# Polysketch attention and an ELU MLP: batch 2's x as products of 64 rows, and the keys' features of batches 2 and 3 in the runs of the queries

## The chip, the cores and the metric

The kernel runs on one core of a Trainium2 chip. The time is that of one execution on the device, in microseconds (us). Profiles show the same execution engine by engine: TensorE (PE) for matmuls, VectorE (DVE), ScalarE (ACT), GpSimd (POOL), and the queues that issue transfers, SyncE's (SP) above all.

## The reference

Four batches, four heads, 1088 tokens, 32 values a head; everything is fp32. Attention is linear: each key and query is turned into 64 features, the outer product of two projections with 8 values each.

```python
def phi(x):                               # S1, S2: 8 x 32
    a = einsum('rd,bhsd->bhsr', S1, x)
    b = einsum('rd,bhsd->bhsr', S2, x)
    return einsum('bhsi,bhsj->bhsij', a, b).reshape(..., 64)

q_p, k_p = phi(q), phi(k)
kv  = einsum('bhsf,bhsd->bhfd', k_p, v)
z   = sum(k_p, axis=2)
num = einsum('bhsf,bhfd->bhsd', q_p, kv)
den = einsum('bhsf,bhf->bhs', q_p, z)[..., None] + 1e-06
x   = (num / den) as 4352 tokens x 128     # (B*S, H*D)
h   = x @ w_in                             # 128 x 2048
out = where(h > 0, h, exp(min(h, 0)) - 1) @ w_out   # 2048 x 128
```

## The kernel before

**Stages.** Each batch's keys become features (`KF`), their outer products (`KO`, `KO_a`, `KO_b`), and the sums over the tokens `kv` and `z` (`KA`, `Z`). `KT_out` sends `kv` through DRAM into the layouts in which the queries need it: `kvs` (32 rows a tile, the two halves of the features apart) or `kv2` (64 rows a tile). The queries become features (`q1`, `q1_out`), are multiplied and divided by the denominator (`q2_...`), are turned (`q4`), and give x by a product with `kv` (`q5`, `q5_out`).

**The MLP.** The tokens are worked in units `g` of 512 (0 to 7; the last, 8, has 256). Units 2 and 3 are called group 2, 4 and 5 group 4, 6 and 7 group 6; group 8 is the small rest. For each unit there are eight steps `cp` over w_in's columns: `mm1` (L259, tile `h`, two halves of 128 columns), `elu_a` on ACT (L930 RELU, L932 EXP), `elu_d` on DVE (L938, writes `gg`), then the second product, `mm2` for unit 0 and `mm2_seven` (L839) from unit 1 on. `mm2_seven` forms a 2x2 block product from seven products instead of eight; the sums that it needs of `gg` are made by POOL (`sums7`, L795, L800, L802), those of the weights once by `weights7`. Column tiles are 32 wide at first and 64 wide once `width[0] = 64` is set.

**Queries beside the MLP.** `queries(g5s, g1s, step)` takes the two `h` tiles of a step `(unit, cp)` before the step's own `mm1` needs them, and two more PSUM banks, and puts into the four of them x of the groups `g5s` and the features of the groups `g1s`. A group in `pairs` has its x made by `q5_pairs` (L738): 16 matmuls on tiles of 64 rows x 32 columns with `kv2`, from a tile of queries that `q4` has turned on DVE and exchanged between partitions with eight DMAs for each of its halves. Any other group has it made by `q5` (L726): two times 16 matmuls on tiles of 32x32 that add up (f = 0, 1), one half of the features each; a `q1` of the same run stands between them. `q1` (L574) is 16 matmuls on 32x32 tiles. Reading the banks is left to `q5_out` (ACT, L749) and `q1_out` (DVE, L589).

**Keys' features.** `KF_late` (L366) makes those of one batch as eight matmuls on 64x32 tiles with 288 columns each, in two banks of their own; `KF_late_out` (L376) turns each bank with one DVE transposition of 288 columns. Batches 2 and 3 are made in one place, one of them in the two `h` tiles of a step.

**Order.** It is written out by hand, some 880 lines of calls. Each engine executes its instructions in the order in which these calls record them; an instruction waits by semaphores for what it reads, and for a buffer to come free. From unit 6 on, a loop writes the rest. The PSUM tiles `h` have four buffers, two a step.

The calls around the places that are moved, before: group 2's queries and x, and the keys' features.

```python
queries((), (2,), (1, 4))
...
queries((2,), (), (2, 0))
...
queries((), (4, 8), (3, 1))
...
queries((4,), (6,), (3, 7))
```

Of the kernel before, what the change touches and what calls it, by code (L numbers as in the profile page):

```python
# [29 lines left out]
def kernel(  # L30
# [326 lines left out]
    def KF_late(b, step=None):  # L357
        if step is None:
            ps = [psum.tile([P, 512], F32, name="kfps", tag="aux") for _ in range(2)]
        else:  # L360
            ps = hs[step] = [psum.tile([P, 512], F32, name="h", tag="h", bufs=4) for c in range(2)]
        for c in range(4):
            u, w = divmod(c, 2)
            for g2 in range(2):
                r = slice(64 * g2, 64 * g2 + 64)
                nc.tensor.matmul(ps[g2][32 * c:32 * c + 32, :32 * KT],  # L366
                                 Sxp[r].rearrange("p x c r -> p (x c r)"),
                                 kT[b][r, u * KT:u * KT + KT, 32 * w:32 * w + 32],
                                 skip_group_check=True, tile_position=(64 * g2, 32 * c))
        feats[b] = ps  # L370

# [379 lines left out]
    def queries(g5s, g1s, step):  # L751
# [10 lines left out]
        for g, c in keys:  # L762
            q1(g, ps, c, c > 0)
        for g, c in sums:
# [256 lines left out]

    transp(kT, "k", 0, 2, 5)
    KF_first((0, 0), (1, 0))
    KF_first((2, 0), (3, 0))
    transp(kT, "k", 0, KT, KT + 5)
# [3 lines left out]
    transp(kT, "k", 0, 5, KT)  # L1029
    KF_first((5, 0), (3, 1))  # L1030
    KF_first((6, 0), (4, 1))
    KF_first_out(0)
    transp(kT, "k", 0, KT + 5, NT)
    KF_first((5, 1), (7, 0))
    KF_first((6, 1), (8, 0))
    KF_first((7, 1), (8, 1))
    KF_first_out(1)
    KF_first_out(2, slice(1, 2))
    KF_first_out(2, slice(0, 1))
    transp(qT, "q", 0, 0, 8)  # L1040
# [60 lines left out]
    elu_a(0, 0, 0, (0,))
    R1(strip, 4)
    q2_rec(1)
    R1(floor, 4)
    q2_an(1)
    R1(shift, 4)
    whole_half(0, 1)
    R1(whole, 1)
    mm1_first(1, (0, 1))
    elu_a(0, 0, 0, (1,))  # L1110
    q2_out(1, 1)
    mm1(0, 1, (1,))
    mm1(0, 1, (0,))
    q4_early(1, 1)
    R1(round_s, 4)
    q2_out(1, 0)
    elu_d(0, 0, 0)
    elu_a(0, 0, 1, (0,))
    q4_early(1, 0)
    elu_a(0, 0, 1, (1,))  # L1120
    elu_a(0, 1, 1, (0,))
    elu_a(0, 1, 1, (1,))
    elu_d(0, 0, 1)
    R1(whole, 4)
    mm1(0, 2, (0,))
    mm1(0, 2, (1,))
    R1(floor, 2)
    R1(shift, 2)
    R1(round_s, 2)
    q4_out(1, 1)  # L1130
    q4_out(1, 0)
    R1(strip, 7)
    elu_d(0, 1, 1)
    KT_out(0)
    elu_a(0, 1, 0, (0,))
    R1(floor, 3)
    R1(strip, 5)
    R1(whole, 2)
    elu_a(0, 2, 1, (0,))
    elu_a(0, 1, 0, (1,))  # L1140
    q5_early(1)
    q5_early_out(1, 1)
    q5_early_out(1, 0)
    mm2(0, 0, False, (0,))
    R1(shift, 3)
    R1(floor, 5)
    R1(low, 5)
    R1(round_s, 3)
    elu_a(0, 2, 1, (1,))
    R1(shift, 5)  # L1150
    R1(whole, 3)
    weights7(slice(1, 2), 0)
    mm2(0, 0, False, (1,))
    elu_a(0, 2, 0, (0,))
    elu_a(0, 2, 0, (1,))
    elu_d(0, 1, 0)
    R1(floor, 7)
    mm1(1, 0, (1,))
    mm1(1, 1, (0,))
    elu_d(0, 2, 1)  # L1160
    mm1(1, 0, (0,))
    R1(round_s, 5)
    elu_a(1, 1, 0, (0,))
    elu_a(1, 1, 0, (1,))
    R1(strip, 6)
    elu_d(0, 2, 0)
    R1(strip, 8)
    R1(floor, 6)
    R1(shift, 6)
    R1(floor, 8)  # L1170
    R1(round_s, 6)
    R1(whole, 5)
    elu_a(1, 0, 0, (0,))
    elu_a(1, 0, 0, (1,))
    R1(low, 6)
    elu_a(1, 0, 1, (0,))
    R1(shift, 7)
    mm2(0, 1, False, (0,))
    elu_a(1, 0, 1, (1,))
    R1(low, 7)  # L1180
    elu_d(1, 0, 0)
    mm2(0, 1, False, (1,))
    mm2(0, 2, False, (0,))
    mm2(0, 2, False, (1,))
    transp(kT, "k", 1, 9, NT)
    R1(shift, 8)
    R1(round_s, 7)
    mm1(1, 1, (1,))
    elu_a(1, 1, 1, (0,))
    elu_a(1, 1, 1, (1,))  # L1190
    R1(low, 8)
    transp(kT, "k", 1, 0, 9)
    elu_d(1, 0, 1)
    R1(whole, 6)
    mm2_blocks(0, (0,))
    mm1(0, 3, (0,))
    R1(low, 9)
    elu_d(1, 1, 1)
    R1(strip, 9)
    elu_d(1, 1, 0)  # L1200
    KF_late(1, None)
    R1(strip, 10)
    R1(round_s, 8)
    elu_a(0, 3, 0, (0,))
    elu_a(0, 3, 0, (1,))
    elu_d(0, 3, 0)
    R1(whole, 7)
    mm1(0, 3, (1,))
    elu_a(0, 3, 1, (0,))
    mm1(0, 4, (1,))  # L1210
    mm2_blocks(0, (1,))
    elu_a(0, 3, 1, (1,))
    mm1(0, 4, (0,))
    elu_a(0, 4, 0, (0,))
    elu_d(0, 3, 1)
    elu_a(0, 4, 0, (1,))
    KF_late_out(1, 1)
    weights7(slice(2, 4), 0)
    make_SWs()
    R1(floor, 10)  # L1220
    R1(floor, 9)
    R1(shift, 10)
    elu_d(0, 4, 0)
    R1(shift, 9)
    transp(kT, "k", 2, 0, 9)
    R1(round_s, 9)
    mm2(0, 3, False, (0,))
    mm2(0, 3, False, (1,))
    R1(whole, 8)
    mm1(0, 5, (0,))  # L1230
    mm1(1, 2, (1,))
    mm1(0, 5, (1,))
    R1(whole, 9)
    elu_a(0, 4, 1, (0,))
    elu_a(0, 4, 1, (1,))
    elu_d(0, 4, 1)
    KF_late_out(1, 0)
    elu_a(0, 5, 0, (0,))
    KO(1, 0, nc.gpsimd)
    mm2(0, 4, False, (0,))  # L1240
    mm2(0, 4, False, (1,))
    elu_a(0, 5, 1, (0,))
    elu_a(0, 5, 1, (1,))
    elu_d(0, 5, 1)
    elu_a(0, 5, 0, (1,))
    elu_d(0, 5, 0)
    KO_a(1, 1)
    KO_b(1, 1)
    R1(round_s, 10)
    transp(qT, "q", 1, 0, 9)  # L1250
    mm1(0, 6, (0,))
# [24 lines left out]
    elu_a(0, 6, 1, (1,))
    elu_d(1, 2, 1)
    Z_out(1, kv_ps[1])
    Z_share(1)
    elu_d(0, 6, 1)  # L1280
    elu_d(1, 2, 0)
    sums7(1, 2, 0)
    weights7(slice(1, 2), 2)
    mm1(0, 7, (0,))
    elu_a(0, 7, 0, (0,))
    elu_a(0, 7, 0, (1,))
    mm2(0, 6, False, (0,))
    mm2(0, 6, False, (1,))
    mm1(0, 7, (1,))
    transp(kT, "k", 3, 0, 9)  # L1290
    elu_a(0, 7, 1, (0,))
    elu_d(0, 7, 0)
    sums7(1, 1, 1)
    weights7(slice(0, 1), 0)
    weights7(slice(1, 2), 3)
    sums7(1, 1, 2)
    transp(kT, "k", 3, 9, NT)
    queries((), (2,), (1, 4))
    mm1(1, 3, (0,))
    q1_out(2, (2,))  # L1300
    mm2(0, 7, True, (0,))
    q1_out(2, (1,))
    weights7(slice(4, 8), 0)
    elu_a(0, 7, 1, (1,))
    elu_d(0, 7, 1)
    q1_out(2, (3,))
    mm2(0, 7, True, (1,))
    mm1(1, 4, (1,))
    q1_out(2, (0,))
    q2_prod(2)  # L1310
    elu_a(1, 3, 0, (0,))
# [4 lines left out]
    fin1(0)
    q2_sum(2)
    sums7(1, 2, 1)
    weights7(slice(4, 8), 2)
    q2_rec(2)  # L1320
    elu_a(1, 4, 1, (0,))
    q2_an(2)
    mm1(1, 6, (1,))
    mm1(1, 4, (0,))
    elu_a(1, 3, 1, (1,))
    elu_d(1, 3, 1)
    elu_a(1, 4, 0, (0,))
    mm2_seven(1, 1, True, False)
    q2_half(2, 0)
    elu_a(1, 4, 0, (1,))  # L1330
    elu_d(1, 4, 0)
    weights7(slice(2, 4), 3)
    elu_a(1, 4, 1, (1,))
    elu_d(1, 4, 1)
    weights7(slice(2, 4), 2)
    weights7(slice(4, 8), 1)
    mm1(1, 6, (0,))
    elu_a(1, 6, 0, (0,))
    elu_a(1, 6, 1, (0,))
    elu_a(1, 6, 0, (1,))  # L1340
    elu_a(1, 6, 1, (1,))
    sums7(1, 2, 2)
    mm2_seven(1, 2, False, False)
    mm1(1, 5, (0,))
    mm1(1, 5, (1,))
    sums7(1, 3, 0)
    sums7(1, 3, 1)
    q2_half(2, 1)
    weights7(slice(4, 8), 3)
    elu_a(1, 5, 0, (0,))  # L1350
    elu_a(1, 5, 1, (0,))
    elu_a(1, 5, 1, (1,))
    elu_d(1, 6, 1)
    sums7(1, 3, 2)
    elu_d(1, 6, 0)
    sums7(1, 4, 0)
# [617 lines left out]
```

## Time and profile before

| | us |
|---|---|
| three runs | 259.96, 260.21, 260.28; median 260.21 |
| the profiled execution | 260.24, its span 258.3 |
| PE busy | 251.9 (98%) |
| POOL, ACT, DVE busy | 183.9, 182.1, 175.6 |
| first product of the MLP starts | 16.10 |
| TensorE's granted clock | 1.0 throughout |

The span is the time between the first and the last instruction of the profile; 1.9 us of the measured time lie outside of it. Busy times of the engines overlap. PE's is modelled at its ends, so that neighbouring matmuls overlap in the views by some tenths of a us; the chain of waits shows them without the overlap.

### The profile page before, as it was taken

Reading aid. Unit: us, or ns where it says so; the run is one execution under the profiler, and the core shown is the slowest. Engines: PE = TensorE matmul, PEld = TensorE weight load, DVE = VectorE, ACT = ScalarE, POOL = GpSimd, SP = SyncE. Lnnn points to the kernel's source line nnn. Section 1 sums busy time; section 2 is a strip of 40 time slices with the busy share of each in tenths; the row PEclk is TensorE's granted clock in tenths of the full one; section 3 lists DMA queues with packets and bytes.
Section 4 is the critical chain, followed back from the end, with each engine's and each line's share of the span. In section 5 each row is a group of like instructions: output and inputs, shape, how many; then the busy total and the mean of one; then the engine's idle time right before and its main releaser. Section 6 shows DMA issues by size and latency. Waiting matters only on the chain.

```text
span 258.3 us, 9815 instructions
## 1 busy us (share of the span) xinstructions
PE 251.9 (98%) x4133; PEld 160.0 (62%) x4133; DVE 175.6 (68%) x342; ACT 182.1 (70%) x357; POOL 183.9 (71%) x236
## 2 busy tenths in 40 slices
PE   8789999999999999999999999999999999999994
PEld 7643333426666677567566666666766666667994
DVE  5799998898859875789665678743455445644641
ACT  2589887748757657667687777578777777777792
POOL 5433365698994978875779877987888888888310
PEclk9999999999999999999999999999999999999999
DMA  6999692303000111100110004321021100110021
GB/s 187 288 348 248 203 279 59 93 20 52 14 5 4 22 26 27 24 5 5 25 18 3 3 1 95 86 43 28 12 30 25 20 3 0 22 24 3 3 32 31
DMA packets 30427, 15.61 MB, mean 60 GB/s; under 512 B 22544, under 2 KB 28048, under 8 KB 30384
## 3 DMA queue, kind: packets, MB, share of 16 engines
q1 hardware_dynamic: 29520, 14.22, 23.2%
q10 hardware_dynamic: 800, 0.71, 1.0%
q8 instruction: 32, 0.52, 0.8%
q14 instruction: 11, 0.09, 0.1%
q0 software_dynamic: 64, 0.07, 0.1%
HBM read 11.31 MB, written 2.36 MB: 53 GB/s over the span
## 4 chain that ended last, share of the span: by engine, by line
PE 95%; DMA 2%; issue 1%; ACTq 1%; DVE 0%; ACT 0%; DVEq 0%
PE h L259 46%; PE pb L839 18%; PE pa L839 15%; PE o L259 5%; PE ol L259 3%; DMA hd_q<-in_q_dram 2%; PE kv L453 1%; PE qtp L640 1%; PE h L574 1%; PE h L726 1%; PE pb L815 1%; PE xps L666 1%; PE kv L439 1%; PE kfps L366 1%; PE h L738 0%
## 5 line engine op out<-in xcount | busy, mean ns | idle before, releaser
L938 DVE SCALAR_TENSOR_TENSOR gg<-e,h 128x512 f32<-128x512 f32 x128 | 85.4, 683 | 59.7 <-ACT e L932 42.2
L259 PE MATMUL h<-xg,W 128*32 128x512 f32 (+2 forms) x768 | 121.5, 584 | 0.7 <-DVE xg L678 0.7
L930 ACT ACTIVATE e<-h 128x512 f32<-128x512 f32 x128 | 75.0, 591 | 52.4 <-PE h L259 50.4
L795 POOL TENSOR_TENSOR tt<-gg 128x512 f32<-128x512 f32 x55 | 71.6, 1301 | 26.6 <-DVE gg L938 21.1
L932 ACT ACTIVATE e<-e 128x512 f32<-128x512 f32 x128 | 79.0, 630 | 3.0
L259 PEld LDWEIGHTS h<-xg,W 128*32 128x32 f32 (+1 forms) x768 | 34.2, 119 | 44.4 <-issue 32.2
L800 POOL TENSOR_TENSOR tt<-tt,gg 128x256 f32<-128x256 f32 x55 | 41.7, 759 | 3.1
L802 POOL TENSOR_TENSOR tt<-gg,tt 128x256 f32<-128x256 f32 x55 | 40.7, 744 | 3.1
L839 PEld LDWEIGHTS pa<-gg,W 128*64 128x64 f32 (+1 forms) x528 | 25.8, 125 | 25.5 <-issue 25.2
L839 PE MATMUL pa<-gg,W 128*64 128x128 f32 (+1 forms) x528 | 32.4, 273 | 0.0
L839 PE MATMUL pb<-tt,SS 128*64 128x128 f32 (+1 forms) x472 | 29.5, 273 | 0.0
L145 POOL TENSOR_TENSOR W<-W,raw 128x256 uint32<-128x256 uint32 (+2 forms) x12 | 11.7, 978 | 20.0 <-DVE W L119 8.3
L839 PE MATMUL pa<-tt,SS 128*32 128x128 f32 (+1 forms) x404 | 25.3, 273 | 0.0
L839 PEld LDWEIGHTS pb<-tt,SS 128*64 128x64 f32 (+1 forms) x472 | 22.7, 127 | 0.0
L839 PE MATMUL pb<-gg,SS 128*64 128x128 f32 (+1 forms) x292 | 21.9, 273 | 0.0
L839 PE MATMUL pb<-tt,W 128*64 128x128 f32 (+1 forms) x292 | 21.9, 273 | 0.0
L839 PEld LDWEIGHTS pa<-tt,SS 128*32 128x32 f32 (+1 forms) x404 | 17.0, 120 | 0.0
L259 PE MATMUL o<-gg,W 128*32 128x512 f32 x128 | 15.3, 593 | 0.0
L839 PEld LDWEIGHTS pb<-gg,SS 128*64 128x64 f32 (+1 forms) x292 | 13.9, 124 | 0.0
L839 PEld LDWEIGHTS pb<-tt,W 128*64 128x64 f32 (+1 forms) x292 | 13.9, 124 | 0.0
L991 DVE SCALAR_TENSOR_TENSOR gg<-e,h 128x256 f32<-128x256 f32 x16 | 6.6, 418 | 6.4 <-PE h L259 3.2
L259 PEld LDWEIGHTS o<-gg,W 128*32 128x32 f32 x128 | 4.1, 110 | 9.3 <-issue 7.1
(181 smaller groups left out, 273.3 us busy)
## 6 DMA issues: line engine op xcount, KB each, us to landing
raw<-in_moe_w_in_dram SPq DMA_DIRECT2D x8, 256.0 KB, 6.0
raw<-in_moe_w_out_dram SPq DMA_DIRECT2D x8, 256.0 KB, 5.7
out_dram<-ob SPq DMA_DIRECT2D x112, 16.0 KB, 1.5
hd_k<-in_k_dram SPq DMA_DIRECT2D x3, 544.0 KB, 8.5
hd_q<-in_q_dram SPq DMA_DIRECT2D x3, 544.0 KB, 10.0
v<-in_v_dram SPq DMA_DIRECT2D x4, 288.0 KB, 10.0
raw<-qpF SPq DMA_DIRECT2D x16, 64.0 KB, 2.0
v<-in_v_dram SPq DMA_DIRECT2D x3, 256.0 KB, 10.0
```

The source lines that it names most:

```text
L145: nc.gpsimd.tensor_tensor(dst.bitcast(U32), dst.bitcast(U32), words(raw)[0], op=ADD)
L259: nc.tensor.matmul(dst[c:c + tile], lhs[:, c:c + tile], rhs, skip_group_check=True, tile_position=(0, c), **kw)
L366: nc.tensor.matmul(ps[g2][32 * c:32 * c + 32, :32 * KT], Sxp[r].rearrange("p x c r -> p (x c r)"), kT[b][r, u * KT:u * KT + KT, 32 * w:32 ...
L439: nc.tensor.matmul(kv_ps[0][32 * h:32 * h + 32, :R * R], vt[0][:, (h * KT + i) * D:(h * KT + i + 1) * D], feats[0, i // 5][:, i % 5, h].re ...
L795: nc.gpsimd.tensor_tensor(_ap(ts[g, cp][:, 0], [[4 * P, 2], [P, 2], [1, P]]), _ap(gs[g, cp][:, 0, P:], [[4 * P, 2]] + us), _ap(gs[g, cp][: ...
L800: nc.gpsimd.tensor_tensor(t[:, 1], t[:, 2], quarter(g, cp, 0, 0), op=ADD)
L802: nc.gpsimd.tensor_tensor(t[:, 3], quarter(g, cp, 1, 0), t[:, 1], op=SUB)
L839: nc.tensor.matmul(bank[r:r + width[0], P * col:P * col + P], lhs[:, w:w + width[0]], rhs[:, u], start=(first and i in ((0,) if g == 1 els ...
L930: nc.scalar.activation(e, hs[g, cp][c][:, :n], RELU, scale=-1.0)
L932: nc.scalar.activation(e, e, EXP, scale=-1.0)
L938: nc.vector.scalar_tensor_tensor(gs[g, cp][:, c, :n], es[g, cp][:, c, :n], -1.0, hs[g, cp][c][:, :n], op0=ADD, op1=MAX)
L991: nc.vector.scalar_tensor_tensor(gs["last", k // 2][:, k % 2, :2 * P], es["last", k // 2][:, k % 2, :2 * P], -1.0, hs["last", k][:, :2 * P ...
```

## The change

Four things are changed.

1. `pairs` holds group 4 too: batch 2's x is made by `q5_pairs`, and `KT_out` writes no `kvs` for batch 2.
2. `KF_beside` makes the features of batch 3's keys in the run of group 2's queries (step (1, 4)) and those of batch 2's keys in the run of group 2's x (step (2, 0)), in columns 256 and up of the same four banks: 16 matmuls with 160 or 128 columns on 64x32 tiles, in place of eight with 288. `KF_beside_out` turns them in four transpositions instead of two.
3. The queries of groups 4 and 8 are made in the run of step (2, 7) instead of (3, 1).
4. The whole order is written anew. Of what it moves, the text speaks of these: `q4_early(1, 1)` and `q4_early(1, 0)` (the `qtp` transpositions, L640) no longer follow each other on PE but have a `mm1` between them, and so have the two halves of `KA(1)`; `KS_turn` and `KS_out` come earlier at the start; `width[0] = 64` is set before the run of step (3, 7) and not behind it; only one `mm1` stands between that run and `mm1(3, 7, (0,))`.

```diff
-    pairs = (6, 8)
+    pairs = (4, 6, 8)
...
-    kvs = {b: const.tile([P, H, 2, D], F32, name=f"kvs{b}") for b in (1, 2)}
+    kvs = {b: const.tile([P, H, 2, D], F32, name=f"kvs{b}") for b in (1, )}
...
+    def KF_beside(b, ps):
+        feats[b, "kf"] = ps
+        feats[b] = work.tile([P, 2, KT, H, R], F32, name="abk", tag="abk", bufs=2)
+        for c in range(4):
+            u, w = divmod(c, 2)
+            for i in range(4):
+                g2, (t0, t1) = i // 2, ((0, 5), (5, KT))[i % 2]
+                r = slice(64 * g2, 64 * g2 + 64)
+                nc.tensor.matmul(ps[i][32 * c:32 * c + 32, 256:256 + 32 * (t1 - t0)],
+                                 Sxp[r].rearrange("p x c r -> p (x c r)"),
+                                 kT[b][r, u * KT + t0:u * KT + t1, 32 * w:32 * w + 32], start=False, stop=True,
+                                 skip_group_check=True, tile_position=(64 * g2, 32 * c))
+
+    def KF_beside_out(b, i):
+        g2, t = i // 2, (slice(0, 5), slice(5, KT))[i % 2]
+        nc.vector.transpose(feats[b][:, :, t, 2 * g2:2 * g2 + 2, :].rearrange("p x t c r -> p t x (c r)"),
+                            feats[b, "kf"][i][:, 256:256 + 32 * (t.stop - t.start)].rearrange(
+                                "p (t x y) -> p t x y", x=2, y=2 * R))
...
-    def queries(g5s, g1s, step):
+    def queries(g5s, g1s, step, kf=None):
...
             q1(g, ps, c, c > 0)
+        if kf:
+            KF_beside(kf, ps)
         for g, c in sums:
...
+    queries((), (2,), (1, 4), 3)
...
+    mm1(1, 4, (0,))
...
+    mm1(1, 7, (1,))
...
+    queries((2,), (), (2, 0), 2)
+    q5_out(2, 0, 0)
+    q5_out(2, 1, 0)
...
+    KF_beside_out(2, 3)
...
+    mm1(1, 7, (0,))
+    elu_a(1, 7, 0, (0,))
+    q5_out(2, 0, 1)
...
+    KF_beside_out(2, 1)
+    KF_beside_out(2, 0)
...
+    mm2_seven(1, 5, False, False)
+    KF_beside_out(2, 2)
+    mm1(2, 0, (0,))
...
+    queries((4,), (6,), (3, 7))
+    mm1(3, 6, (0,))
...
+    q5_out(4, 0, 0)
+    elu_a(3, 6, 1, (0,))
+    q1_out(6, (0,))
+    mm1(3, 7, (0,))
```

More of the change, by code (lines that the diff above doesn't have):

```diff
@@ L1114 @@
     q4_early(1, 1)
-    R1(round_s, 4)
+    elu_a(0, 0, 1, (0,))
+    R1(low, 2)
+    elu_a(0, 0, 1, (1,))
+    mm1(0, 2, (0,))
+    make_SWs()
     q2_out(1, 0)
-    elu_d(0, 0, 0)
-    elu_a(0, 0, 1, (0,))
+    elu_d(0, 0, 1)
+    q4_out(1, 1)
+    R1(whole, 2)
     q4_early(1, 0)
-    elu_a(0, 0, 1, (1,))
+    R1(floor, 3)
+    R1(strip, 5)
+    elu_a(0, 1, 0, (0,))
+    elu_a(0, 1, 0, (1,))
+    q4_out(1, 0)
+    mm2(0, 0, False, (0,))
+    KT_out(0)
+    mm2(0, 0, False, (1,))
+    R1(floor, 5)
@@ L1121 @@
+    R1(shift, 3)
+    elu_a(0, 2, 0, (0,))
+    R1(strip, 6)
+    R1(low, 5)
+    elu_a(0, 2, 0, (1,))
+    R1(round_s, 3)
+    R1(strip, 7)
+    elu_d(0, 1, 0)
+    q5_early(1)
+    mm1(0, 2, (1,))
+    R1(shift, 5)
+    R1(floor, 6)
+    q5_early_out(1, 1)
+    q5_early_out(1, 0)
+    R1(whole, 3)
+    mm2(0, 1, False, (0,))
+    mm1(1, 1, (0,))
     elu_a(0, 1, 1, (0,))
     elu_a(0, 1, 1, (1,))
[L1123 to L1127, printed above, removed]
@@ L1161 @@
     mm1(1, 0, (0,))
[L1162 to L1181, printed above, removed]
     mm2(0, 1, False, (1,))
     mm2(0, 2, False, (0,))
+    mm1(1, 1, (1,))
@@ L1211 @@
[L1211 to L1227, printed above, removed]
+    elu_a(1, 1, 1, (1,))
+    elu_a(0, 3, 1, (1,))
+    R1(low, 8)
+    weights7(slice(1, 2), 0)
+    R1(round_s, 8)
@@ L1297 @@
[L1297 to L1311, printed above, removed]
+    elu_d(1, 2, 1)
+    transp(kT, "k", 3, 9, NT)
+    transp(kT, "k", 2, 0, 9)
+    elu_d(1, 2, 0)
+    keep_last(1)
+    mm2(0, 6, False, (0,))
@@ L1312 @@
+    elu_a(1, 3, 1, (0,))
+    elu_a(1, 3, 1, (1,))
+    sums7(1, 2, 2)
+    sums7(1, 1, 2)
+    q2_rec(2)
+    elu_d(1, 4, 0)
+    q2_an(2)
+    mm2_seven(1, 1, True, False)
+    elu_d(1, 4, 1)
+    sums7(1, 4, 0)
+    q2_half(2, 1)
+    elu_d(1, 3, 1)
     elu_a(1, 3, 0, (1,))
-    mm1(1, 3, (1,))
-    elu_a(1, 3, 1, (0,))
     elu_d(1, 3, 0)
[L1316 to L1343, printed above, removed]
@@ new lines @@
+    elu_a(2, 5, 1, (0,))
+    KA(3, (1,))
+    sums7(2, 3, 1)
+    Z_share(2)
+    sums7(2, 3, 2)
+    sums7(2, 4, 1)
+    elu_a(2, 5, 0, (1,))
+    elu_a(2, 5, 1, (1,))
+    elu_d(2, 5, 0)
+    elu_a(2, 6, 1, (0,))
+    elu_d(2, 5, 1)
+    mm2_seven(2, 3, False, False)
+    elu_a(2, 6, 1, (1,))
+    elu_a(2, 6, 0, (0,))
+    elu_a(2, 6, 0, (1,))
+    sums7(2, 5, 0)
+    KT_out(3)
+    zls[3] = ZC(3, kv_ps[3])
+    Z(3, kv_ps[3], zls[3])
+    Z_out(3, kv_ps[3])
+    elu_d(2, 6, 0)
+    elu_d(2, 6, 1)
@@ L1649 @@
+    q2_prod(8)
+    q2_an(6)
+    elu_d(3, 7, 1)
     elu_d(3, 7, 0)
-    elu_d(3, 7, 1)
-    sums7(3, 5, 1)
+    mm1(4, 0, (1,))
+    mm1(4, 0, (0,))
+    elu_a(4, 0, 1, (0,))
+    q5_out(4, 1, 1)
     sums7(3, 5, 2)
-    elu_a(3, 6, 0, (0,))
-    mm1(4, 0, (1,))
-    elu_a(3, 6, 0, (1,))
-    elu_d(3, 6, 0)
-    q2_sum(6)
+    mm2_seven(3, 5, False, False)
     sums7(3, 6, 0)
+    elu_a(4, 0, 1, (1,))
+    elu_d(4, 0, 1)
     sums7(3, 6, 1)
-    sums7(3, 7, 0)
-    elu_a(4, 0, 1, (0,))
-    q2_rec(6)
@@ L1738 @@
-    sums7(4, 3, 2)
-    mm1(4, 6, (1,))
-    elu_d(4, 4, 1)
-    q2_sum(8)
+    elu_d(4, 4, 1)
+    elu_d(4, 4, 0)
+    sums7(4, 7, 0)
+    mm1(4, 5, (1,))
+    mm1(4, 6, (1,))
+    elu_a(4, 6, 1, (0,))
+    elu_a(4, 5, 1, (0,))
+    mm1(4, 5, (0,))
+    mm2_seven(4, 3, False, False)
+    mm1(4, 6, (0,))
+    elu_a(4, 5, 0, (0,))
+    sums7(4, 7, 1)
+    fin_seven_c(3)
+    q2_rec(8)
+    q2_an(8)
+    q2_half(8, 0)
+    elu_a(4, 5, 0, (1,))
     sums7(4, 4, 0)
-    elu_a(4, 6, 1, (0,))
-    elu_a(4, 6, 1, (1,))
+    sums7(4, 7, 2)
@@ new lines @@
+    elu_a(5, 3, 0, (0,))
+    sums7(5, 2, 1)
+    sums7(5, 1, 2)
+    mm2_seven(5, 1, False, False)
+    elu_a(5, 3, 1, (0,))
+    elu_a(5, 3, 0, (1,))
+    elu_d(5, 4, 0)
+    elu_d(5, 3, 0)
+    sums7(5, 2, 2)
+    mm2_seven(5, 2, False, False)
+    elu_a(5, 3, 1, (1,))
+    queries((6, 8), (), (5, 7))
+    q5_out(6, 0, 1)
+    q5_out(6, 1, 0)
+    q5_out(8, 0, 0)
+    q5_out(6, 0, 0)
+    q5_out(8, 0, 2)
+    q5_out(8, 0, 1)
+    mm1(5, 5, (1,))
+    elu_a(5, 5, 1, (0,))
+    elu_d(5, 3, 1)
@@ L1848 @@
+    elu_a(5, 5, 1, (1,))
+    sums7(5, 3, 0)
+    sums7(5, 3, 1)
+    sums7(5, 3, 2)
+    mm1(5, 5, (0,))
+    q5_out(8, 0, 3)
+    sums7(5, 4, 0)
+    elu_a(5, 5, 0, (0,))
+    mm1(5, 7, (1,))
+    mm1(5, 7, (0,))
+    mm2_seven(5, 3, False, False)
+    elu_d(5, 5, 1)
+    mm1(5, 6, (1,))
+    elu_a(5, 5, 0, (1,))
+    fin_seven_c(4)
+    elu_d(5, 5, 0)
     sums7(5, 5, 0)
-    sums7(5, 3, 0)
-    queries((6, 8), (), (5, 7))
-    elu_d(5, 4, 0)
+    sums7(5, 4, 1)
+    elu_a(5, 7, 0, (0,))
+    q5_out(6, 1, 1)
```

1063 lines of the change are left out of this document (506 added, 557 removed).

## The prediction

> **What bounds the kernel now.** I read the page's shares and its chain first.
>
> ```profile
> PE 251.9 (98%) x4133; PEld 160.0 (62%) x4133; DVE 175.6 (68%) x342; ACT 182.1 (70%) x357; POOL 183.9 (71%) x236
> ...
> PE 95%; DMA 2%; issue 1%; ACTq 1%; DVE 0%; ACT 0%; DVEq 0%
> ```
>
> TensorE carries the chain. The view of waits, for PE, says whether it ever stands:
>
> ```profile
> PE kv L439 <- issue: 0.8, 1, 0.8
> PE idle L267 <- PEq L1959: 0.8, 1, 0.8
> PE h L259 <- DVE xg L678: 0.7, 1, 0.7
> PE abqp L527 <- DVE qT L285: 0.5, 1, 0.5
> ```
>
> All four lie before the first product of the MLP, which starts at 16.10. From there on PE has no gap. So three things can move the end: the start, what PE loses where the shape of its tiles changes, and new waits. The matmuls are the same work: counted from the two built programs, columns by share of the array, they agree.
>
> The chain (start, us, what) prices a change of shape:
>
> ```profile
> 19.75 1.02 PE qtp L640 x8
> 20.77 1.85 PE h L259 x16
> ...
> 33.66 0.65 PE kfps L366 x16
> ...
> 43.89 1.72 PE h L259 x16
> ...
> 73.19 0.86 PE h L259 x8
> 74.05 0.65 PE kfps L366 x16
> 74.69 0.48 PE h L366 x16
> 75.18 0.99 PE h L259 x8
> ```
>
> Sixteen `h` take 1.72 in a row of their own shape and 1.85 behind another; eight take 0.86 and 0.99. So each return costs 0.13. `qtp` streams as many columns as eight `h` and takes 1.02 instead of 0.86, so entering it costs about 0.16. The runs of `queries` are read in the same way, from the end of one neighbour to the start of the next:
>
> ```profile
> 52.88 0.34 PE h L574 x2
> ...
> 53.54 0.55 PE h L259
> ...
> 70.09 0.34 PE h L726 x2
> ...
> 71.52 0.36 PE pa L839 x8
> ...
> 122.18 0.34 PE h L726 x2
> ...
> 124.24 1.00 PE h L259 x3
> ```
>
> "Bare" below is columns alone, at the rate of the long products (512 columns in 0.86, four 32-wide or two 64-wide tiles at once; the sixteen tiles of 32x32 work together). Group 2's q1, one set of 16 matmuls: 0.66 (bare 0.43). Group 2's x, two sets: 1.43 (bare 0.85). Step (3, 7) with group 4's two sets and group 6's one: 2.06 (bare 1.28). The excess is 0.23, 0.58, 0.78 for one, two, three sets. Step (3, 1), two sets: 104.66 to 105.82, 1.16 (bare 0.53, excess 0.63). Groups 6 and 8 as pairs: 176.31 to 177.71, 1.40 (bare 1.07, excess 0.33), group 6's part 0.88.
>
> **The change, part by part,** from the profiled execution of 260.24 (span 258.3 and 1.9 around it; the median is 0.03 less).
>
> Start. The first KA waits for v's landing, whose issue is not moved; KA is at 10.03 in both. Behind it, KS_turn and KS_out come earlier, so that `xps` (14.70) waits less: about -0.06. ACT's strip(2) now stands ahead of KS_out and waits for a weight that lands at 12.54; about 0.15 us are to spare.
>
> Keys' features. Removed: KF(2)+KF(3), 74.05 to 75.18, 1.13, and the 0.13 of the `h` behind it. Added: in the run of steps (1, 4) a second set (bare 0.43+0.48=0.91), in that of (2, 0) a set between two (bare 1.33), and one and two changes between 32x32 and 64x32 tiles, which the trace does not show. By the excess of two and three sets: 0.91+0.33 to 0.91+0.63 is 1.24 to 1.54, and 1.33+0.58 to 1.33+0.78 is 1.91 to 2.11. An inner change costs between nothing and 0.15 (the `qtp` row). I take 1.50 and 2.20, since a set of another shape must wait for its weights too. Together 3.70 against 0.66+1.43+1.13+0.13=3.35: **+0.35** (-0.20 to +0.75).
>
> Batch 2 as pairs. Step (3, 7) has two sets instead of three: 0.88 (group 6's row) + 0.66 (q1's row) + 0.15 = 1.69 against 2.06: **-0.37** (-0.52 to 0). The widening of the column tiles moves ahead of the run; I take nothing for it, 0.13 at most.
>
> `q4_early(1, ·)` is cut in two by a product: one more entry and one more return, 0.16+0.13: **+0.30**. KA(1) is cut in two; a half behind a product starts about 0.1 late (45.61+0.86=46.47, first `kv` at 46.59): **+0.08**. Steps of q1(4) and q1(8) only change their step: nothing.
>
> The Trainium skill, "TensorEngine Tiling (Array Packing)", Key Properties, says that changing the tiling mode drains TensorE. By that rule the five changes more that I count from the first product on would cost 5 x 0.29/2 = 0.7 by the `qtp` row before anything is saved; the rows above agree that a change costs, and the sum here has them one by one.
>
> Waits that are new. PE stands only if a bank is not read in time, so I walked the outputs of each run.
>
> ```profile
> 71.56 0.37 ACT L749 COPY xg<-qps 128x256 f32<-128x256 f32 x1 [0.52 <-PE qps L726]
> 71.83 0.66 ACT L749 COPY xg<-h 128x256 f32<-128x256 f32 x2
> ...
> 124.27 0.65 ACT L749 COPY xg<-h 128x256 f32<-128x256 f32 x2 [0.76 <-PE qps L726]
> ```
>
> DVE's reading of a bank waits for ACT's reading of the same one (at 124.95 it starts 0.03 behind the copies). In (2, 0), KF_beside_out(2, 1) waits for q5_out(2, 0, 1), and that stands on ACT behind the RELU of mm1(1, 7, (0,)). From that product's end: RELU starts 0.21 later, the copy 0.50 after it and takes 0.39, then two transpositions (0.30 and 0.32, between the 0.21 of 64 columns and the 0.42 of 256, overlapping by 0.06) and 0.12 for two handovers: 1.78. mm1(2, 0, (0,)) needs that bank, and PE gets there after one mm2_seven, 1.50: **+0.28** (0 to 0.5). Queued behind are the ELU of (1, 7) and, through it, mm1(2, 1). In (3, 7) one product instead of two stands between the run and mm1(3, 7, (0,)): copy 0.22 to 0.61 after the run, transposition to 1.08, PE there at 0.98: **+0.13**. In (1, 4) four transpositions fit with 0.3 to spare, and in (5, 7) the copies with 0.3.
>
> Off PE. Batch 2's x now goes through SP: 16 DMAs in q4(4) (the page has 64 KB, 2.0 us each), for four fewer in KT_out(2), which were done long before. SP first issues 16 outputs of fin_seven_c(1) (0.6 each), then eight pieces at 0.45 and, after the other q4(4), eight more: landed about 121.5, needed at 124; 2.3 us of cover. POOL's sums7, 1.36+0.81+0.69 a product from when the ELU is there, keep 0.5 us before their use at the tightest (mm2_seven(5, 4)); that of before keeps 0.4. No cost.
>
> Sum: -0.06+0.35-0.37+0.30+0.08+0.28+0.13 = +0.71, so 260.95; I say **260.9**. 0.2% is 0.52 us, about what a measurement can tell from no change, so 259.7 to 260.7 counts as the same.
>
> **Rivals.**
> *DVE late at 60 to 70 us* (slower still). Its queue from 58.9: q2_rec 0.35, seven ELU writes at 0.65, q2_an 0.5, two products of 1.22, two transpositions of 1.24, one KF output 0.25: 10.6 to 11.3 us. elu_d(1, 5, 1) is ready about 68.8 for mm1(1, 7, (1,)) at 69.5, elu_d(1, 5, 0) at 70.0 for the run at 70.5. Half a microsecond late decides it, and then it is paid one to one, 0.5 to 1.5: 261.4 to 262.4. Against it: PE is itself later by then.
>
> *The sets refill each other's time* (the other side). If the excess is PE waiting for the next set's weights, a set of long passes between two others hides it: then each run keeps one set's 0.23, 0.91+0.23=1.14 in (1, 4) and 1.33+0.23=1.56 in (2, 0), and (3, 7) is 0.88 and a bare 0.43, 1.31: -0.65 and -0.75 instead of +0.35 and -0.37. That is -0.67, and -1.08 if the two bank waits go as well: 259.2 to 259.6. For it: 16 KF matmuls behind 16 others took 0.48 (74.69), bare. Against: those had the same shape.
>
> *The change doesn't do what it says*: KF_beside writes a tile twice in a row, and if matmuls start only in written order, the other tiles stand idle behind it: eight tile turns of about 0.37 instead of 0.48 in all, +2.6 a run, 266. Against it, each matmul here is two passes on one tile, and at 176.24 eight tiles start together though the first one's second pass starts at 176.48.
> The Trainium skill, "TensorE: Matmul & The Clock Gate", Part 2, says that "the MATMULs themselves stay in program order"; by that the 266 would come; the 176.24 row speaks against it.
>
> *q4(4) lands after 124*: each microsecond over the 2.3 is paid, 262 to 263. *The small sizes come out low and the bank waits don't show*: 260.2.
>
> **Numbers.** Forecast (260.5 to 261.4) 0.45, DVE 0.16, refill 0.19, small 0.14, order 0.02, DMA 0.04. Left out are the order case, the lower half of refill, and the far ends of DVE and DMA, some 0.2 in all: 259.4 to 262.2. Faster is refill with a little of small, 0.20; same is the rest of small and a quarter of the forecast, 0.24; slower 0.56.
>
> **What would show it.** After, the runs of (1, 4) and (2, 0) as 1.5 and 2.2 in the chain, (3, 7) as 1.7, a `qtp` of four twice with an `h` between, and in the waits of PE two rows more: `h` on DVE `abk`, about 0.3, and on DVE `abw`, about 0.1. Wrong would be: no such row, or runs near 1.2 and 1.6 (then refill), or a wait on `gg` at 69 (DVE), on `raw` at 124 (DMA).

## The result and the profile after

The changed kernel takes 263.06 us (median of 6 executions, 262.00 to 264.11) beside 260.07 for the kernel before (median of 6, 259.05 to 260.28): a ratio of 1.0126, 95% interval 1.0107 to 1.0145. It is slower, as forecast, but by 3.0 us and not by 0.7, and it lies outside the range of 259.4 to 262.2. A second set of executions of the same kernel (r1 below) gave 1.0145 (1.0120 to 1.0169). Each ratio is to the kernel before as it ran in the same set; it is estimated from the executions and need not be the quotient of the two medians. Some executions run in a slower state of the chip, whatever the kernel (two of r5's ten, one of r8's twelve); medians and ratios leave them out.

The profiled execution took 264.11, the slowest of the six, its span 262.0; the granted clock is 1.0. The page's shares, the chain's shares and the waits of PE, after:

```profile
PE 254.3 (97%) x4133; PEld 163.6 (62%) x4133; DVE 175.6 (67%) x346; ACT 180.6 (69%) x357; POOL 184.6 (70%) x236
...
PE 93%; DMA 2%; DVE 1%; ACT 1%; issue 1%; ACTq 1%; DVEq 0%
```

```profile
PE abqp L546 <- DVE qT L285: 1.0, 1, 1.0
...
PE h L259 <- DVE gg L959: 0.6, 1, 0.6
...
PE pb L860 <- issue: 0.3, 1, 0.3
```

The number of matmuls is the same. PE is still the chain, but DVE and ACT have now a share of it, and there are two waits behind the start that the kernel before does not have. The first product of the MLP starts at 16.03 (before 16.10), so from there to the end of the span it is 245.97 against 242.2: 3.8 us more. All of the loss in this execution is behind the start. In r1's profile of the same kernel the same stretch is 245.2, 3.0 us more than before, so the table below shows a loss on the large side.

The predicted parts can be read from the chain and from PE's timeline. The split `q4_early(1, ·)`, from the chain:

```profile
19.86 0.59 PE qtp L659 x4
20.45 0.99 PE h L259 x8
21.44 0.59 PE qtp L659 x4
22.03 1.85 PE o L259 x16
```

Both `qtp` runs pay their entry and both products behind them their return. The runs with the keys' features, by the first matmul of the run and of what follows it, from PE's timeline (start, us, engine, line, instruction):

```profile
51.49 0.41 PE L593 MATMUL h<-qT,SWs 32*32 32x256 f32 x2
...
52.96 1.07 PE L259 MATMUL o<-gg,W 128*32 128x512 f32 x8
```

```profile
70.55 0.41 PE L745 MATMUL h<-qpT,kvs 32*32 32x256 f32 x2
...
72.67 1.07 PE L259 MATMUL h<-xg,W 128*32 128x512 f32 x8
```

That is 1.47 for (1, 4) and 2.13 for (2, 0). In the same way (3, 7) is 126.67 to 128.48, 1.80.

What the sum did not have is elsewhere. First, step (4, 0), in the chain:

```profile
129.60 0.60 ACT e L951
...
130.49 1.12 DVE abw L608 x3
...
132.10 0.47 DVE den L624
...
132.86 0.64 DVE gg L959
133.54 1.94 PE h L259 x8
```

`mm1(4, 0, (1,))` needs a bank of step (3, 6), which `elu_d(3, 6, 0)` reads. That stands on DVE behind `q1_out(6, ·)`, `q2_prod(6)`, `q2_sum(6)` and `q2_rec(6)`, and those wait for ACT, which copies x only behind the RELU of the product at 128.55. PE loses 0.78. Then the weight loads, whose rows name waits that the view of PE's waits leaves out (PEld is TensorE's loading of weights; in brackets: idle time before the row, and what ended it):

```profile
67.80 0.16 PEld L860 LDWEIGHTS pb<-tt,W 128*32 128x32 f32 x8 [0.24 <-POOL tt L823]
...
75.36 0.19 PEld L259 LDWEIGHTS h<-xg,W 128*32 128x32 f32 x8 [0.36 <-ACT e L953]
...
104.32 0.12 PEld L860 LDWEIGHTS pb<-tt,W 128*32 128x32 f32 x3 [0.51 <-issue]
```

The one at 75.36 is the predicted bank wait of (2, 0), though ACT's EXP is named and not DVE's `abk` (whose transposition ends at 75.25). The other two were not foreseen. And SP, which issues the outputs of unit 3 ahead of the last eight DMAs of `q4(6, 1)`:

```profile
152.00 5.06 SPq L736 DMA_DIRECT2D raw<-qpF  x8
157.16 8.76 SPq L922 DMA_DIRECT2D out_dram<-ob  x16
166.01 4.95 SPq L736 DMA_DIRECT2D qpE<-qpF  x8
171.06 5.96 SPq L736 DMA_DIRECT2D raw<-qpF  x8
```

The last of them is issued by 177.02 and lands at 178.47; the run of (5, 7) goes from 177.43 to 179.49, 2.05 instead of 1.40.

| behind the first product, us | predicted | after |
|---|---|---|
| keys' features (3.35 before) | +0.35 | 1.47+2.13-3.35 = +0.25 |
| run (3, 7) (2.06 before) | -0.37 | 1.80-2.06 = -0.26 |
| `q4_early` cut in two | +0.30 | +0.29 |
| `KA(1)` cut in two | +0.08 | +0.06 |
| bank wait in (2, 0) | +0.28 | +0.28 |
| bank wait in (3, 7) | +0.13 | +0.12 |
| change of width before the run (3, 7) | 0 | +0.11 |
| `mm1(4, 0, (1,))` waits for DVE | - | +0.78 |
| run (5, 7) waits for `q4(6, 1)` | - | +0.65 |
| gap inside `mm2_seven(2, 4)`, at 104 | - | +0.65 |
| gap behind the small `Z` product, at 99 | - | +0.33 |
| `mm1` from 16 to 20, `mm2_seven(1, 3)` waits for POOL | - | +0.18, +0.17 |

The first six come to 0.74, the rest to 2.9, together 3.6 of the 3.8.

Two of these rows hang together. Behind the gap at 104 the four column tiles, 32 columns wide each, are out of step: until the change of width at 124 one of them runs 0.14 ahead of the other three.

```profile
120.65 0.59 PE L259 MATMUL h<-xg,W 128*32 128x512 f32 x1
...
120.79 1.89 PE L259 MATMUL h<-xg,W 128*32 128x512 f32 x15
```

From the first matmul of `mm2_seven(3, 2)` (122.36) to the first 64-wide product (124.14) it is 1.78. In r4, r5 and r12, which have no gap at 104, it is 1.64, and such an `mm2_seven` alone takes 1.53. So the change of width itself costs 0.11, and 0.14 there belong to the gap. From the end of the run of (2, 7) to that product it is 21.78, and 21.13 in r12: the gap costs 0.65 in all.

### The profile page after: what moved, and what is told of

It reads as the page before. It is cut to its first block, busy times and chain, and to the rows that moved or that the text cites. A ratio compares the mean times of both kernels' runs of the same rounds, so it can differ in the third digit from the quotient of the medians.

```text
span 262.0 us, 9850 instructions
## 1 busy us (share of the span) xinstructions
PE 254.3 (97%) x4133; PEld 163.6 (62%) x4133; DVE 175.6 (67%) x346; ACT 180.6 (69%) x357; POOL 184.6 (70%) x236
## 4 chain that ended last, share of the span: by engine, by line
PE 93%; DMA 2%; DVE 1%; ACT 1%; issue 1%; ACTq 1%; DVEq 0%
PE h L259 45%; PE pb L860 18%; PE pa L860 14%; PE o L259 5%; PE ol L259 3%; DMA hd_q<-in_q_dram 2%; PE kv L472 1%; PE qtp L659 1%; PE h L757 1%; PE h L593 1%; PE pb L836 1%; PE xps L685 0%; PE kv L458 0%; DVE abw L608 0%; PE h L745 0%
## 5 line engine op out<-in xcount | busy, mean ns | idle before, releaser
L259 PEld LDWEIGHTS h<-xg,W 128*32 128x32 f32 (+1 forms) x768 | 37.0, 119 | 46.6 <-issue 31.5
L860 PEld LDWEIGHTS pa<-gg,W 128*64 128x64 f32 (+1 forms) x528 | 27.5, 125 | 23.1 <-issue 22.0
L860 PE MATMUL pa<-gg,W 128*64 128x128 f32 (+1 forms) x528 | 33.4, 273 | 0.0
L860 PE MATMUL pb<-tt,SS 128*64 128x128 f32 (+1 forms) x472 | 30.6, 273 | 0.0
L860 PE MATMUL pa<-tt,SS 128*32 128x128 f32 (+1 forms) x404 | 26.4, 273 | 0.0
L860 PEld LDWEIGHTS pb<-tt,SS 128*64 128x64 f32 (+1 forms) x472 | 23.7, 127 | 0.0
L860 PE MATMUL pb<-tt,W 128*64 128x128 f32 (+1 forms) x292 | 23.3, 273 | 0.3 <-issue 0.3
L860 PEld LDWEIGHTS pa<-tt,SS 128*32 128x32 f32 (+1 forms) x404 | 18.1, 120 | 0.0
L259 PE MATMUL h<-xgl,W 128*64 128x128 f32 x128 | 9.4, 273 | 0.0
```

Source lines behind the costliest of these rows:

```text
L259: nc.tensor.matmul(dst[c:c + tile], lhs[:, c:c + tile], rhs, skip_group_check=True, tile_position=(0, c), **kw)
L860: nc.tensor.matmul(bank[r:r + width[0], P * col:P * col + P], lhs[:, w:w + width[0]], rhs[:, u], start=(first and i in ((0,) if g == 1 els ...
```

## Experiments

The theory: the terms of the sum are right, and the rest is a set of separate waits that the new order makes on queues far from the edits, each of which goes away when its one call is put elsewhere. The rivals, run by run: that a wait only moves to the next place, that the loss lies in the edits (pairs, keys' features), or that it lies in the start.

### The changed kernel again

> The changed kernel once more, for a second profile and as the ruler of this set. Theory A (new waits, not the new products, make the time): the same three gaps on TensorE come back, 0.78 us ahead of mm1(4, 0, (1,)) at about 133, 0.65 in the run of step (5, 7) at about 178, and some 0.3 and 0.5 around the run of step (2, 7) at 101 and 104; 262 to 264. Theory B (the profile of the first run caught a disturbed execution): one or more of these gaps is gone, and the time is near 262.

Measured: 263.45, ratio 1.0145 (1.0120 to 1.0169). The wait at (4, 0) is there with 0.79, the run of (5, 7) is 1.80 (0.40 over), the gap in `mm2_seven(2, 4)` 0.31. The gap of 0.33 at 99 is not there: that one is a matter of the execution. So is the 0.18 that `mm1` loses from 16 to 20: r6, in the old order, has it too, and r2, r4, r8, r9 and r11, in the new one, do not.

### fin_seven_c(3) behind q4(6, 1)

```diff
-    fin_seven_c(3)
...
     q4(6, 1)
...
+    fin_seven_c(3)
```

> Only fin_seven_c(3), whose 16 output transfers stand on SyncE's queue ahead of the last 16 transfers of groups 8 and 6, is moved behind them. Theory A: the run of step (5, 7) takes 1.40 us again, as in the kernel before, instead of 2.05; 0.65 less than the changed kernel, about 262.4. Theory B (the run is long because of its products, or TensorE waits for something else there): 2.05 stays, no change of the time.

Measured: 264.18, ratio 1.0163 (1.0112 to 1.0214). SP now takes the exchange first:

```profile
165.72 4.94 SPq L736 DMA_DIRECT2D qpE<-qpF  x8
170.76 6.03 SPq L736 DMA_DIRECT2D raw<-qpF  x8
176.89 5.22 SPq L922 DMA_DIRECT2D out_dram<-ob  x9
```

The run of (5, 7), now from 178.63, takes 1.41. This profile alone does not settle it: the last eight DMAs are issued by 176.79, only 0.2 earlier than in the profile after, while PE comes to the run 1.2 later. r5 below has the same order on SP, and its first product starts at 16.39, near the 16.03 of the profile after:

```profile
168.82 6.18 SPq L736 DMA_DIRECT2D raw<-qpF  x8
```

There they are issued by 175.00, two us earlier, and the run takes 1.41 although PE comes to it earlier, at 176.69: the wait was SP's order. The time of r2 shows nothing of it, and in the profiled execution the start says why. The first product starts at 17.85, 1.8 later than in the profile after (behind it, it is 244.7): PE stands 2.2 for q's first rows, and from 10 to 14 us the clock is granted at 0.73, 0.50, 0.50 and 0.57.

### The denominators of group 6 behind elu_d(3, 6, ·)

```diff
-    q2_prod(6)
-    q2_sum(6)
-    q2_rec(6)
     elu_d(3, 6, 0)
...
     elu_d(3, 6, 1)
+    q2_prod(6)
+    q2_sum(6)
+    q2_rec(6)
```

> Only the three instructions of group 6's denominator (q2_prod, q2_sum, q2_rec: 0.42, 0.45, 0.35 us on VectorE) are moved behind elu_d(3, 6, 0) and elu_d(3, 6, 1). Theory A: TensorE no longer waits ahead of mm1(4, 0, (1,)), 0.6 to 0.8 us less than the changed kernel, about 262.3. Theory B: the wait there has another cause (the copies of ScalarE, POOL's sums) and stays over 0.5.

Measured: 262.57, ratio 1.0122 (1.0096 to 1.0149); in the profile behind the first product 244.7, 1.3 less than after. PE's wait on `gg` is gone, since DVE writes it 1.4 earlier:

```profile
131.43 1.28 DVE L959 SCALAR_TENSOR_TENSOR gg<-e,h 128x512 f32<-128x512 f32 x2
```

Not all of the 1.3 is the edit's: the gap at 99 is missing and (5, 7) waits only 0.22, while the gap in `mm2_seven(2, 4)` was 0.80 here. By the times alone the edit is not told apart from none, since the intervals overlap.

### r4_three_waits: both, and elu_d(2, 6, ·) ahead of Z_out(3)

```diff
-    Z_out(3, kv_ps[3])
     elu_d(2, 6, 0)
     elu_d(2, 6, 1)
+    Z_out(3, kv_ps[3])
```

> Both edits, and elu_d(2, 6, 0) and elu_d(2, 6, 1) ahead of Z_out(3) on VectorE, which waits for TensorE. Theory A: the gaps at (5, 7), (4, 0) and 0.3 at (2, 7) are gone, 1.7 us less than the changed kernel, 261.3, and what is left over the kernel before is near the 0.7 of the prediction plus 0.5. Theory B: less than 0.8 comes back; the rest lies in the products and in the changes of shape.

Measured: 261.66, ratio 1.0072 (1.0048 to 1.0096). This interval lies below that of the changed kernel. The waits at (4, 0) and (5, 7) and the gap at 104 are gone together, and in the profile it is 243.4 behind the first product, 1.1 over the kernel before. So most of the unforeseen 2.9 is these. But the start is late in this profile (first product at 17.74), which gives DMAs time. r5, with the same three edits and a start 1.35 earlier, waits 0.66 in the run of (3, 7): a part of what is removed can come back at the next transfer.

### r12: elu_d(2, 6, ·) ahead of Z_out(3) alone

> The changed kernel with one edit: elu_d(2, 6, 0) and elu_d(2, 6, 1) stand ahead of Z_out(3) on VectorE. Theory A (these two free the banks of step (2, 7), and Z_out(3) holds them 1.45 us while it waits for kv): the gap of 0.33 before the run at 101 is gone, the run starts when the product ahead of it ends, and the gap of 0.3 to 0.8 inside mm2_seven(2, 4) goes with it or moves; behind the first h 0.3 to 0.9 below the changed kernel's 245.97. Theory B (both gaps are TensorE waiting for its instructions): the gaps stay where they are, within 0.1 us of their place, and no difference behind the first h.

Measured: 262.51, ratio 1.0095 (1.0063 to 1.0127); behind the first product 244.6. The loads of `mm2_seven(2, 4)` now follow each other without a gap:

```profile
103.00 0.24 PEld L860 LDWEIGHTS pb<-tt,W 128*32 128x32 f32 x8
103.22 0.24 PEld L259 LDWEIGHTS h<-xg,W 128*32 128x32 f32 x8
```

All five profiles without this edit and with the new order (after, r1, r2, r3, r9) have the gap at the same instruction, 0.3 to 0.8; all six with it (r4, r5, r8, r10, r11, r12) have none. The edit removes it, but how is open. The reason that I gave, the bank that `Z_out(3)` holds up, would put the gap before the run, and it lies behind it, where the profile names no releaser. In the five profiles with the gap, a 16 KB instruction packet on the DMA queues ended 1.30 to 1.48 before PE went on, however long the gap was; in the six without it, PE came to the same instruction 1.73 to 2.23 behind the end of such a packet. That PE waits there for its instructions fits both, and is only argued. The gap at 99 is another thing: it was gone here, but r10 and r11 have it with the same edit (0.33 and 0.40), so the edit is not what took it away.

### r5_start_order: the start as before

r4 with `q1_first` again between the calls of `Z_first`, and `q1_first_out` and `q2_out(0, 1)` again behind `zl` and `Z_out`.

> The changed kernel with the three edits of the run before, and TensorE's order at the start put back: the sums of the first keys (Z_first) stand around the queries' first products (q1_first) instead of behind them, and the copy zl on ScalarE ahead of the copy of the queries' features. Theory A (the start hangs on the landing of hd_q since the change, with no time to spare, and where that is late TensorE's clock falls too): the first product of the MLP starts at 16.1 or earlier in the profile, no clock below 1.0 between 10 and 14 us, and the median is 0.4 to 1 us below the run with the three edits, about 261.0. Theory B (the start varies for reasons that the order has no part in): no difference, 261.7.

Measured: 262.1, ratio 1.0078 (1.0052 to 1.0104), against r4's 1.0072. No gain. In the profile, (3, 7) took 2.46: PE comes there at 126.09, and the last DMA of group 4's exchange lands at 127.07 (after: 126.67 and 126.90).

### r9_start_both: the start alone

```diff
-    q1_first(0, 1)
-    q1_first(2, 3)
-    q1_first_out()
     Z_first(0, 1, 2)
+    q1_first(0, 1)
     Z_first(3, 4, 5)
     Z_first(6, 7, 8)
+    q1_first(2, 3)
...
-    q2_out(0, 1)
...
     Z(0, feats["z"], zl)
...
+    q1_first_out()
+    q2_out(0, 1)
...
-    R1(strip, 4)
...
     q5_early_out(0, 1)
+    R1(strip, 4)
```

> The changed kernel with only the start put back: Z_first around q1_first as before, zl ahead of the copy of q1_first, and R1(strip, 4) behind q5_early_out(0, 1). Theory A (the start has no slack against the landing of q's first rows, so in some executions TensorE stands about 2 us and the granted clock then falls to a half): first h at 15.4 to 16.1, no slice of the clock below 0.9 before it, kv x40 at 0.70, and a ratio 0.3 to 0.8 us (0.001 to 0.003) below that of the changed kernel (1.0126 and 1.0145), while the waits behind the start stay: behind the first h 245 to 246. Theory B (the start varies as much in the order of before): same ratio as the changed kernel within 0.0015.

Measured: 263.28, ratio 1.0124 (1.0092 to 1.0157), that of the changed kernel. Theory A falls: with this order too, PE stood 2.2 for q's first rows, the first product started at 16.67, and this time the clock stayed at 1.0. Over all profiles the transposition of those rows starts between 6.8 and 8.4, in both orders. The start scatters with their landing, and it is not where the change loses.

### r6_pairs_only: the kernel before with pairs = (4, 6, 8)

```diff
-    pairs = (6, 8)
+    pairs = (4, 6, 8)
...
-    kvs = {b: const.tile([P, H, 2, D], F32, name=f"kvs{b}") for b in (1, 2)}
+    kvs = {b: const.tile([P, H, 2, D], F32, name=f"kvs{b}") for b in (1, )}
```

> The kernel before with group 4 in pairs and nothing else: batch 2's x in products of 64 rows, in the old order. Theory A (this part gains what its row says): the run of step (3, 7) takes 1.80 instead of 2.06, and the kernel is 0.2 to 0.3 us faster than before. Theory B (16 transfers more on SyncE's queue cost what the products gain): the run waits for the exchanged queries, and the kernel is as before or slower by up to 1 us.

Measured: 268.66, ratio 1.0337 (1.0299 to 1.0375). In the old order the exchange lands far too late, and PE waits for it:

```profile
PE h L738 <- DMA raw<-qpF: 3.6, 1, 3.6
...
PE qps L738 <- DMA raw<-qpF: 1.1, 2, 0.7
```

The 3.6 lie ahead of the run: it begins at 125.79, before at 122.11. Then it takes 6.03 instead of 2.06, with the clock granted at 0.66, 0.50 and 0.50 in the 2 us windows from 126 to 132, and the four products behind it take 4.45 instead of 3.58. That is 8.5 of the 8.8 that it takes longer behind the first product. SP issues the exchange from 116.91 to 128.04. So this rival, the DMAs of `q4(4)`, is real and large; only the new order, in which group 4's queries and their exchange come earlier, keeps it away.

### r7_beside_only: the kernel before with KF_beside in the two runs

```diff
-    queries((), (2,), (1, 4))
+    queries((), (2,), (1, 4), 3)
...
-    queries((2,), (), (2, 0))
+    transp(kT, "k", 2, 9, NT)
+    queries((2,), (), (2, 0), 2)
...
-    transp(kT, "k", 2, 9, NT)
-    KF_late(2, None)
-    KF_late(3, (2, 1))
```

> The kernel before with the keys' features of batches 3 and 2 in the runs of steps (1, 4) and (2, 0) and nothing else. Theory A (this part costs what its rows in the changed kernel say): the runs take 1.47 and 2.13, the run of 1.13 at 74 and its return of 0.13 are gone, so 0.27 slower than before, if VectorE's transpositions are in time. Theory B (the products beside the queries gain, and it is the new order alone that costs): 0.3 us faster than before or more.

Measured: 260.35, ratio 1.0028 (1.0004 to 1.0052), the four `KF_beside_out` placed behind the runs. Behind the first product 242.6, 0.3 over the kernel before; the runs take 1.55 and 2.13. So the profile bears out the predicted +0.35 by itself; the times alone put it between 0.1 and 1.4.

### r8_all_waits: r5 and five small edits

```diff
-    mm1(0, 2, (0,))
...
     q4_early(1, 0)
+    mm1(0, 2, (0,))
...
-    weights7(slice(4, 8), 3)
...
     sums7(1, 3, 2)
+    weights7(slice(4, 8), 3)
...
     q5_out(2, 1, 0)
+    q5_out(2, 0, 1)
...
-    q5_out(2, 0, 1)
...
-    width[0] = 64
...
     queries((4,), (6,), (3, 7))
+    width[0] = 64
...
-    mm1(3, 7, (0,))
...
     mm2_seven(3, 4, False, False)
+    mm1(3, 7, (0,))
```

> The run with the old start, and six smaller edits of the order: q5_out(2, 0, 1) ahead of the RELU of (1, 7); mm1(3, 7, (0,)) behind mm2_seven(3, 4); the two q4_early(1, ·) together again; weights7(slice(4, 8), 3) behind sums7(1, 3, ·); the widening of the column tiles behind the run of (3, 7). Theory A (the loss is a list of waits and changes of shape, each with its price: 0.28, 0.12, 0.29, 0.17, 0.25): 1.1 us below the run with the old start, within 0.3 of the kernel before. Theory B (the new forms of the products cost more than their rows show): it stays 0.7 us or more above the kernel before.

Measured: 260.80, ratio 1.0034 (1.0013 to 1.0056). The edits made are the five that the expectation lists. The bank waits, the change of width ahead of the run and the cut `q4_early` are gone. Behind the first product it is 243.5 all the same, no less than in r4, because three waits have taken their place. PE is now ahead of group 4's exchange: the run (3, 7) takes 2.61 instead of 1.80, with a wait on `raw` that the profile after does not have. The wait on POOL has only moved, from `mm2_seven(1, 3)` to `mm2_seven(1, 4)`, where it costs 0.15:

```profile
68.38 0.16 PEld L860 LDWEIGHTS pb<-tt,W 128*32 128x32 f32 x8 [0.22 <-POOL tt L823]
```

And the second half of the joined `qtp` comes 0.19 late, behind a product on DVE that now follows an ELU write. Without the 0.8 of (3, 7) it would be 0.4 over the kernel before, and these two waits are most of that.

### r10_best: that exchange earlier on SP

r8 with the 16 outputs of `fin_seven_c(1)` ahead of `q4(4, 1)`, and `R1(strip, 4)` behind `q5_early_out(0, 1)`.

> r8_all_waits with R1(strip, 4) behind q5_early_out(0, 1) and with the 16 outputs of fin_seven_c(1) put ahead of group 4's DMAs on SP. Theory A (r8's step (3, 7) waits for the landing of group 4's q4, because SP issues 16 outputs and then 16 DMAs at 0.63 each): run (3, 7) at 1.80 instead of 2.61, nothing on raw in PE's waits, behind the first h 242.4 to 242.8, ratio 0.995 to 1.001. Theory B (the DMAs take longer because the bandwidth or the rings are shared, not because of SP's order): run (3, 7) stays at 2.4 to 2.6, behind the first h 243.2 to 243.6, ratio as r8's 1.0034.

Measured: 260.82, ratio 1.0040 (1.0017 to 1.0064). The run (3, 7) is 1.80 and nothing waits on `raw`, as theory A has it. The time does not follow: 243.3 behind the first product, 0.2 less than r8. SP's DMAs, r8 (first line) and r10:

```profile
111.66 12.32 SPq L736 DMA_DIRECT2D raw<-qpF  x16
```

```profile
111.97 12.35 SPq L736 DMA_DIRECT2D raw<-qpF  x16
```

They are no earlier. It is PE that comes later, at 125.59 instead of 124.30: 0.64 of it is a later start, 0.33 the gap at 99, some 0.2 a longer wait of `qtp` for DVE, behind which the moved `R1` call may stand (not tried alone). In r10 the first eight begin right when DVE has made their tile (111.95), in r8 1.0 later; the second eight are all issued 5.8 us after DVE has made theirs in r10, and 6.8 in r8. So SP's order was a part of r8's wait, and the long transfers themselves the rest.

### r11_best_no_pairs: r10 without pairs for group 4

```diff
-    pairs = (4, 6, 8)
+    pairs = (6, 8)
...
-    kvs = {b: const.tile([P, H, 2, D], F32, name=f"kvs{b}") for b in (1, )}
+    kvs = {b: const.tile([P, H, 2, D], F32, name=f"kvs{b}") for b in (1, 2)}
```

> r10_best with batch 2's x not in pairs again (pairs 6 and 8, no DMAs in q4(4)). Theory A (the pairs save what the prediction gave them, 0.26 in step (3, 7), and the DMAs cost nothing once they land in time): run (3, 7) at 2.0 to 2.1, 0.2 to 0.3 above r10_best behind the first h. Theory B (the pairs' DMAs still cost something elsewhere, on SP or POOL): no slower than r10_best, or faster by up to 0.3.

Measured: 260.72, ratio 1.0036 (1.0016 to 1.0056), that of r10. The run (3, 7) is 2.06 again, and behind the first product it is 243.6, 0.3 over r10, as theory A says; the median does not show it. The pairs save 0.26 on PE, and the scatter of the start is larger than that. None of these versions beats the kernel before.

## Why the prediction was wrong

**Where it was right.** The six terms that it worked out measured 0.74 behind the start against 0.77 predicted, each within 0.11. Runs (1, 4) and (2, 0) came out at 1.47 and 2.13 (forecast 1.50 and 2.20); r7 alone bears out their sum. The price of entering and leaving another shape, read from `qtp` and `h`, held for the cut `q4_early`. The start's -0.06 is -0.07 in the profile, which is luck as much as order: the start scatters by more than a microsecond with the landing of q's rows. The sum for the bank wait in (3, 7) is off by a little: its 1.08 and 0.98 give 0.10, not 0.13.

**The step that failed** is "Waits that are new": "PE stands only if a bank is not read in time, so I walked the outputs of each run". The walk ended at the banks of the four runs that the change edits. But the whole order was written anew, so every wait between engines was new. The bank that cost most, 0.78 in (4, 0), is one of an ordinary step, read by an ordinary ELU that stood behind group 6's denominators on DVE; r3 takes it away. The place to look for it was also wrong: the two rows named as the signs of the bank waits are not in the view of PE's waits, since those waits stand on weight loads. It is the mechanism of the rival "DVE late at 60 to 70 us", at another place, 60 us on.

**"Off PE ... No cost"** failed twice. The walk of SP's queue covered group 4's DMAs and not group 6's, for which the same question, what SP issues ahead of them, had the answer: 16 outputs. That cost 0.13 to 0.65 in the five profiles with that order, and r2's edit takes it away, as r5 shows. And group 4's cover was put at 2.3 us from an issue time of 0.45 a piece, though SP's timeline of before has 16 of group 6's in 11.05. Here they were issued one every 0.63, with the gap between the halves and some stretched ones 12.6 us in all, the last by 125.45, and landed at 126.90 instead of 121.5. They were in time only because PE was late by then too; r5 and r8, where it is not, wait 0.7 and 0.8. POOL's sums, with "0.5 us before their use at the tightest", were late once, by 0.17, in `mm2_seven(1, 3)`; r8 moves one call of POOL's and only shifts that wait to the next product.

**"I take nothing for it, 0.13 at most"** for the change of width was near: it cost 0.11 ahead of the first 64-wide product and 0.05 in it, 0.16 in all. Taking nothing was a little too low; this is not where the forecast failed.

**The rivals.** Refill: no, the runs keep their excess. Written order: no; (2, 0) would have taken 2.6 more. The Trainium skill, "TensorE: Matmul & The Clock Gate", Part 2, with its matmuls in program order, is not borne out by 1.47 and 2.13 for runs in which each tile is written twice in a row. The Trainium skill, "TensorEngine Tiling (Array Packing)", Key Properties, by which a change of mode drains TensorE, agrees in kind: 0.29 for one entry and one return more, 0.11 for the change of width. The condition of *q4(4) lands after 124* came true, with 126.90, but not its price, because PE itself came to the run at 126.67; r5 and r8 pay a part of it.

**What stays open**: the gaps at 99 and at 104 (0.33 and 0.65 in the profile after), for which the profile names no releaser, and the 0.18 that `mm1` loses from 16 to 20, which comes and goes with the execution in the old order too. Together that is 1.2 of the unforeseen 2.9; no step of the prediction could have given it.

## What to carry to other kernels

When the order of a kernel is rewritten, the edited places are the smaller part of the forecast: list for every product what frees its bank, which instructions now stand ahead of that on its engine, and for every exchange what its queue issues first; three such places (0.78, 0.65 and 0.17) were worth twice the sum of the edits, and three losses without a known releaser 1.2 more. A wait that is removed shows in the run it held up, and shows in the time only as far as the next transfer has slack, so look at both. Keep a piece of the queue's own measured rate (here 0.63 us a transfer) for the transfers that are moved, not the rate of others nearby.

## What the runs showed of the hardware

- The granted clock fell to 0.50 for 3.4 us in r2 and r4 (in r2, 0.73, 0.50, 0.50 and 0.57 in the windows from 10 to 14), shortly after PE had stood 2.2 and 2.1 us near the start; `kv` x40 then takes 1.22 and 0.95 instead of 0.69. In r6 the same came behind the 3.6 us wait for the exchange, for 6.8 us. In r9 PE stood 2.2 as well and the clock stayed at 1.0, so standing for that long does not decide it. The Trainium skill, "TensorE: Matmul & The Clock Gate", Part 1, has the clock halved by an idle window of about 3.4 us that runs freely; the fall to 0.50 agrees, while the stands here are shorter, and no run shows where a window begins.
- Waits of PE on a semaphore stand mostly on the rows of the weight loads. In the profile after, the view of PE's waits listed 0.9 of some 3 us that PE stood behind the start.
- One instruction on DVE was stretched without a visible wait: in the profile after, the 128x1024 product at 64.47 took 1.86, the same one at 60.78 1.21. POOL's sum at 65.33, which overlaps it, took 1.60, the next of its kind at 67.70 0.75; the sum that PE waits for at 67.80 is the one between them. No run tests whether one caused the other.
- A gap on PE can put the column tiles out of step: behind the one at 104 a tile runs 0.14 ahead of the other three for 20 us, and the difference is paid at the change of width (1.78 instead of 1.64).
